# A Hedgehog attention mix on one core: raw K and Q weights by 128-partition transfers of one head per partition block, x0's low parts on VectorE, another order of V and the folds

## The chip, the core and the metric

The kernel runs on one core of a Trainium2 chip. Its engines have their own instruction queues and wait for each other by semaphores: PE (TensorE, matmuls; PEld is its weight load), DVE (VectorE), ACT (ScalarE), POOL (GpSimd), and SP (SyncE), which here only issues DMA transfers. The metric is device time in microseconds (us) of the launch, the median of several runs. The profile shows one further execution.

## The reference

Two attention branches, A and B, get the same `x` (2048 tokens of 448) and are mixed by a gate. All is float32.

```python
qkv = (x @ wqkv) -> q, k, v            # 16 heads of 28
pq, pk = q @ w_phi, k @ w_phi          # per head, 28 x 28
phi(p) = concat([softmax(p), softmax(-p)])
kv = einsum("bhsf,bhsd->bhfd", phi(pk), v);  z = sum over s of phi(pk)
o  = (phi(pq) @ kv) / (phi(pq) @ z + 1e-6)
out_branch = o.reshape(B, S, D) @ wo
g = sigmoid((x * gate_w).sum(-1));  result = g * out_A + (1 - g) * out_B
```

## The kernel before

**Precision.** A product of float32 matrices is made of three faster ones: each operand is split into a rounded high part (fp32r) and a low part, what is left (`low_part`, a subtraction of two SBUF tiles), and high*high, high*low and low*high are summed in PSUM. So each 448-row contraction is 11 matmuls (`mms`), and each projection of one tile of 128 tokens for one branch is a group of 11: VA and VB (V of branch A and B), K and Q.

**Folding.** K and Q are never computed raw. `fold` multiplies the raw weights (transposed, rows = head dimension) with `w_phi` once, so that the projections give the features directly. The raw weights lie in `wts[:, k, b, g]` (k: K or Q; b: branch; g: head within a block), a view of the tile `ret`: block q of four heads lies on the partitions 32q to 32q+27, and each of its four heads g is a row piece of 512 floats. One fold covers two of the four g (gh and gh+2) of one branch, for K and Q: 32 small matmuls of 28 rows into the PSUM tile `F` (the profile has two PE records for each), a 32x32 block transpose of F by DVE (`STREAM_TRANSPOSE`) into `ft` (two buffers, `ret` and `ru` in turn), then the high parts by ACT (rk for K, rq for Q) and the low parts by DVE or POOL. There are four folds, in program order F0 and F1 (branch A), F2 and F3 (branch B); F has one buffer. `wpd`, the other operand of the folds, comes from eight small transfers that POOL issues (`load_wp`).

**Loads.** `load_x0`, `load_wv`, `load_x` and half of `load_wt` are issued by SP in a single queue. The raw V weights are `wvr` (eight transfers, chunk c and branch b). The raw K and Q weights come as 16 transfers, one for each (k, b, q): 28 partitions, on each four pieces of 2 KB. For q = 0, 1 SP issues them, for q = 2, 3 POOL. A transfer waits on SP until the one issued eight before it has landed. The second branch's raw weights share memory with `wvr` and wait until that is read; the third pair of x tiles (`load_x(2)`, called x2 below, tokens 512 to 767) shares `xraw` with x0.

**Order.** `steps()` lists the work in the order that PE has to do it. `Plan.order` takes the cost, the latency and the dependences of each step, works out a due time for each (its lead `ahead` moves it earlier), and lists the instructions of the other engines accordingly; no run-time scheduler is behind it. `two` marks steps of DVE and POOL that the planner doesn't put beside each other.

**The start** is: `v_first` (V of the tiles 0 and 1 from x0, as the chunks of x0 and of the V weights land; V of tile 1 is put into the PSUM tile `K`), then VA and VB of the tiles 2, 3 and 4 with the folds among them, then K and Q of tile 0, K of tile 1, and from there a steady stream of K, Q, V and the accumulation of kv over the 16 tiles. The exponentials and normalisations of K are made by ACT, POOL and DVE (`k_soft`), those of Q after a turn through DRAM (`q_front`, `q_soft`). The last stage computes the numerators (`num`), mixes them and multiplies with `wo`.

**x0.** Chunk 0's low part and the mixed chunk's are made by DVE, those of the chunks 1 and 2 (128x512) by POOL.

Of the kernel before, what the change touches and what calls it, by code (L numbers as in the profile page):

```python
# [7 lines left out]
F32 = mybir.dt.float32  # L8
# [19 lines left out]
class Plan:  # L28
# [5 lines left out]
    def __init__(self):  # L34
        self.steps, self.writer, self.readers = [], {}, {}

    def add(self, eng, cost, fn, r=(), w=(), lat=0.1, kb=0, two=False, ahead=0.0):
# [10 lines left out]
        self.steps.append((eng, cost, lat, fn, deps, kb, two or eng == "POOL", ahead))  # L48

    def hand_over(self, old, new, fn=None):  # L50
        self.add("NONE", 0.0, fn, (), (*old, *new), lat=0.0)
# [56 lines left out]

def steps():

    yield from (("V01", 0, 0, 1), ("x1",), ("V01", 1, 0), ("V01", 1, 1), ("wq", 0), ("x", 2), ("wq", 1), ("V", 2), ("F", 0, 0, "DP"), ("V", 3, 0), ("F", 0, 1, "DP"))
    yield from (("V", 3, 1), ("V", 4, 0), ("F", 1, 0, "DD"), ("V", 4, 1), ("F", 1, 1, "DD"), ("later",), ("k", 0, 0), ("q", 0, 0), ("k", 0, 1), ("ks", 0), ("K", 1), ("wo_rows",))
    yield from (("q", 0, 1), ("qf", 0))
    yield from (("S", 0, JIT % 3 - 1), ("K", 2), ("Q", 1), ("S", 1, (JIT - 1) % 3 - 1), ("k", 3, 0), ("k", 3, 1), ("kv", 0, 1), ("ks", 3), ("V", 5))
    for p in range(2, 8):
        if p < 7:
            yield "x", p + 1
        yield "K", 2 * p
        yield "Q", 2 * p - 2
        if 2 * p - 2 < JIT:  # L120
            yield "S", 2 * p - 2, (JIT - 2 * p + 2) % 3 - 1
        if p == 7:
            yield "V", 14, 0
        yield "kv", 2 * p - 2, 2 * p - 1
        yield "wo", p - 2
        if p in (3,):
            yield "wo", 6
        if p < 6:
            yield "V", 2 * p + 2
        yield "K", 2 * p + 1  # L130
        if p < 7:
            yield "Q", 2 * p - 1
            if 2 * p - 1 < JIT:
                yield "S", 2 * p - 1, (JIT - 2 * p + 1) % 3 - 1
        if p < 6:
            yield "V", 2 * p + 3
        if p == 6:
            yield "gates", 0, 12
            yield "gates_b", 0, 12
    yield from (("load_wo",), ("V", 14, 1), ("Q", 13), ("V", 15), ("free_v",), ("free_k",), ("kv", 14, 15), ("free_e",), ("kv_turn",), ("gates", 12, NT))  # L140
    yield from (("fetch", 0, 2), ("fetch", 1, 3), ("Q", 14))
    kept, late = list(range(2, JIT - 2)), list(range(JIT, NT))
    rest = []
    while kept or late:
        rest.append((kept.pop(0) if kept else late.pop(0), late.pop(0) if late else kept.pop(0)))
    pairs = [((JIT - 1, JIT - 2), (0, 1)), ((0, 1), (2, 3))] + [(t, (2 * (i % 2), 2 * (i % 2) + 1)) for i, t in enumerate(rest)]
    for p, (tiles, slots) in enumerate(pairs):
        yield "num", tiles, slots
        if p == 0:
            yield from (("Q", 15), ("free_x",), ("free_q",))  # L150
        if p:
            for i, t in enumerate(pairs[p - 1][0]):
                yield "out", 2 * p - 2 + i, t, ("O0", "O1")[i]
        end = p == len(pairs) - 1
        yield "mix", p, ("DVE", "DVE") if end else ("POOL", "POOL"), ("T0", "T1"), ("DVE", "DVE") if end else ("POOL", "POOL")
        if p == 1:
            yield "gates_b", 12, NT, [("o", 2)]
        if p + 2 < len(pairs):
            for t, s in zip(*pairs[p + 2]):
                yield ("S" if t >= JIT else "fetch"), t, s  # L160
    for i, t in enumerate(pairs[-1][0]):
        yield "out", 2 * len(pairs) - 2 + i, t, ("O0", "O1")[i]
# [7 lines left out]
def hedgehog_mix(ctx: ExitStack, tc: tile.TileContext, xd, wv, wkt, wqt, wphi, wo, cmask, cpmask, out):  # L170
# [107 lines left out]
    def put(eng, n, fn, r, w, **k):  # L278
        add(eng, both(eng, n), fn, r, w, **k)

    def low_part(eng, n, o, a, h, r, w):
        put(eng, n, tt(eng, o, a, h, OP.subtract), r, w, two=eng == "DVE")

# [11 lines left out]
    def split_x0():  # L295
        n, t, f = 0, xs[0], xs[0].bitcast(F32)
        h, l = [[(k, n, i) for i in range(2)] for k in ("x", "xl")]
        put("ACT", 2 * P, act(t[:, 0], xraw[:, 0]), [("x0raw", 0)], [("x0h", 0)])
        low_part("DVE", 2 * P, t[:, 4], xraw[:, 0], f[:, 0], [("x0raw", 0), ("x0h", 0)], [("x0l", 0)])
        put("DVE", 6 * P, lambda: V.tensor_copy(t[:, 1:4], xraw[:, 1:]), [("x0raw", 1)], [("x0h", i) for i in (1, 2, 3)])  # L300
        low_part("DVE", 2 * P, t[64:P, 3], xraw[64:P, 3], f[64:P, 3], [("x0raw", 1)], [("x0h", 3)])
        low_part("POOL", 4 * P, t[:, 5:7], xraw[:, 1:3], f[:, 1:3], [("x0raw", 1), ("x0h", 1), ("x0h", 2)], [("x0l", i) for i in (1, 2)])

    def load_x(p):
        xraw, kr = raws[p]
        add("SP", 0.4, dma(xraw, xd[:, 2 * P * p:2 * P * p + 2 * P].rearrange("(c p) t -> p c t", p=P)), [], [(kr,)], lat=2, kb=512)

    def split_x(p, lo, hi, low, high="ACT", after=()):
        xraw, kr = raws[p]
# [9 lines left out]

    def load_wv(c, b):  # L320
        lo, hi = ((0, D + 2), (D + 2, 2 * D + 2))[b]
        add("SP", 0.4, dma(wvr[:, c, lo:hi], wv[c * P:(c + 1) * P, lo:hi]), [], [("wvr", c, b)], lat=2.5, kb=331, ahead=50.0 if c + b == 0 else 30.0 - 2 * (c + 4 * b))

    def split_wv(c, b, low):
        lo, hi = ((0, D + 2), (D + 2, 2 * D + 2))[b]
# [24 lines left out]
    def fold(b, gh, low):  # L350
        n = 2 * b + gh
        def mm():
            for l in range(2):
                g = 2 * l + gh
                for o in range(4):
                    for q in range(4):
                        nc.tensor.matmul(bank["F"][32 * o:32 * o + 32, q, 256 * l:256 * l + 256], wpd[32 * q:32 * q + DH, b, g],
                                         wts[32 * q:32 * q + DH, :, b, g].rearrange("p k (j o i) -> p o k j i", o=4, i=32)[:, o],
                                         start=True, stop=True)
        add("PE", 1.4, mm, [("wpd",), *[("wt", k, b, q) for k in range(2) for q in range(4)]], ["F"])  # L360
        f = ft[n % 2]
        add("DVE", 2.25, lambda: V.transpose(f.rearrange("p k j f u -> p (u k j f)"), bank["F"].rearrange("p k n -> p (k n)")),
            ["F"], [ftk[n % 2]], ahead=4.0 * (n == 3))
        for k, (wh, wl) in enumerate(((wkh, wkl), (wqh, wql))):
            for j in (0, 2):
                h, l = (x[:, j:j + 2, b, :, gh::2].rearrange("p j f u -> p j u f") for x in (wh, wl))
                s = f[:, k, j:j + 2, :FD].rearrange("p j f u -> p j u f")
                key = "kq"[k]
                add("ACT", 0.9, act(h, s), [ftk[n % 2]], [(key, "h", b, gh, j)], ahead=2.0 * (k == 0))
                e = "POOL" if low[k] == "P" or low[k] == "M" and j else "DVE"  # L370
                add(e, {"DVE": 0.88, "POOL": 1.4}[e], tt(e, l, s, h.bitcast(F32), OP.subtract), [ftk[n % 2], (key, "h", b, gh, j)], [(key, "l", b, gh, j)], two=e == "DVE")

    def wkeys(k, bs):
        return [(k, h, b, gh, j) for h in "hl" for b in bs for gh in range(2) for j in (0, 2)]
# [309 lines left out]
    def free_q():  # L684
        pools["q"].close()
        banks("three", "right", O1=1, T1=1)

    nums, outs, loaded = [0], [0], {}
    for what, *a in steps():
        if what == "V":  # L690
# [3 lines left out]
            v_first(a[0], a[1:])  # L694
        elif what in ("K", "k", "ks"):
            if what == "k" and a == [0, 0]:
                plan.hand_over([("x1raw",), *[("wt", k, 1, q) for k in range(2) for q in range(4)]], [("e", n, s) for n in range(NE) for s in range(2)])
            if what != "ks":
                for b in a[1:] or range(2):
                    k_proj(a[0], b)  # L700
# [21 lines left out]
        elif what == "x1":  # L722
# [4 lines left out]
        elif what == "wq":  # L727
            if a[0]:
                plan.hand_over([("wvr", c, b) for c in range(4) for b in range(2)], [("wt", k, 1, q) for k in range(2) for q in range(4)])
            for k in range(2):  # L730
                load_wt(k, a[0])
        elif what == "wo":
            split_wo(a[0])
        elif what == "num":
# [73 lines left out]
```

## Time and profile before

| | |
|---|---|
| median of 3 runs | 346.66 us (344.67 to 346.75) |
| the profiled execution | 345.97 us, span 344.2 us |
| busy share of the span | PE 97%, PEld 86%, DVE 83%, POOL 73%, ACT 42% |
| granted TensorE clock, mean | 0.995 |
| HBM read, written | 32.00 MB, 24.22 MB |
| first fold's matmuls, last fold's | 22.06 us, 39.88 us from the span's start |

A line of the timeline is: start in us, length in us, engine, line of the code, operation, out<-in, shapes, count; in brackets the idle time of the engine just before it, and what ended it. Neighbouring instructions of one kind are one row, so a group of 11 matmuls is one row with x11. PE's times are modelled at their ends: successive groups of 11 start 2.2 us apart where nothing holds them. A row of the stages is: from:to, length, then busy time (and count) of PE, PEld, DVE, ACT and POOL, the granted clock, the mean busy share of the 16 DMA engines, and GB/s. KB are of 1024 bytes.

### The profile page before, as it was taken

The numbers are of one execution on the slowest core, as the hardware profiler recorded it, in microseconds if no ns is written. First come the engines' busy times: TensorE is split into PE (matmuls) and PEld (weight loads), VectorE is DVE, ScalarE is ACT, GpSimd is POOL, SyncE is SP. The second block draws the span as 40 slices with busy tenths as digits, with TensorE's granted clock in tenths as the row PEclk, the third lists the DMA queues.
The fourth block names the chain that finished last, engine by engine and source line by source line (L and its number), as shares of the span: only waits on it lengthen the run. The fifth ranks groups of instructions, "written<-read, shape, count | busy, mean of one in ns | idle before, by whom it ended". The sixth has DMA issues, their size and how long they took to land.

```text
span 344.2 us, 8900 instructions
## 1 busy us (share of the span) xinstructions
PE 333.1 (97%) x3776; PEld 296.5 (86%) x3776; DVE 285.1 (83%) x338; ACT 143.7 (42%) x219; POOL 251.5 (73%) x211
## 2 busy tenths in 40 slices
PE   7889899999999999999999999999999999999995
PEld 6777587999999999999999999899878888788894
DVE  4608886997779769899998999997599999999960
ACT  4516743553444535364444452343043243433231
POOL 8426605899999799999996998697087778788500
PEclk9999989999999999999999999999999999999999
DMA  7995620550317756964735422376974545141011
GB/s 251 251 206 133 203 75 1 156 168 2 116 55 261 252 169 229 327 204 197 246 84 236 143 55 81 96 248 261 301 259 164 202 152 183 76 177 55 29 53 53
DMA packets 29262, 55.18 MB, mean 160 GB/s; under 512 B 4472, under 2 KB 23528, under 8 KB 26920
## 3 DMA queue, kind: packets, MB, share of 16 engines
q1 hardware_dynamic: 28328, 52.68, 47.6%
q0 software_dynamic: 896, 1.95, 2.6%
q8 instruction: 29, 0.48, 0.6%
q14 instruction: 9, 0.07, 0.1%
HBM read 32.00 MB, written 24.22 MB: 163 GB/s over the span
## 4 chain that ended last, share of the span: by engine, by line
POOL 30%; PE 24%; DVE 23%; DMA 10%; issue 8%; ACT 2%; SPq 1%; POOLq 0%; DVEq 0%; ACTq 0%
POOL ret L266 20%; PE O L630 10%; DVE ret L545 5%; DMA ret<-in_wqt 4%; PE K L409 3%; POOL rx L266 3%; PE Q L409 3%; DVE rv L593 3%; POOL rv L602 3%; PE N L582 2%; DVE sm L488 2%; DVE mx L481 2%; DVE qsm L540 2%; DMA wst<-wos 1%; DMA ret<-in_wv 1%
## 5 line engine op out<-in xcount | busy, mean ns | idle before, releaser
L409 PE MATMUL K<-rk,rx 128*128 128x432 f32 x352 | 74.0, 366 | 0.7 <-ACT pk L269 0.6
L409 PE MATMUL Q<-rq,rx 128*128 128x432 f32 x352 | 72.4, 360 | 0.2 <-DVE Q L672 0.2
L409 PEld LDWEIGHTS K<-rk,rx 128*128 128x128 f32 x352 | 67.1, 192 | 5.1 <-ACT pk L269 1.5
L630 PE MATMUL O<-rk,rx 128*128 128x448 f32 x336 | 70.6, 369 | 0.1
L630 PEld LDWEIGHTS O<-rk,rx 128*128 128x128 f32 x336 | 62.5, 188 | 8.5 <-ACT rx L621 1.2
L409 PEld LDWEIGHTS Q<-rq,rx 128*128 128x128 f32 x352 | 65.9, 188 | 4.4 <-PE K L409 0.7
L269 ACT ACTIVATE ret<-ret 128x896 f32<-128x896 f32 x48 | 45.7, 953 | 55.0 <-POOL ret L266 54.9
L266 POOL TENSOR_TENSOR ret<-ret,sm 128x896 f32<-128x896 f32 x32 | 53.9, 1707 | 8.1 <-DVE sm L489 8.1
L266 POOL TENSOR_TENSOR ret<-pk,mx 128x896 f32<-128x896 f32 x16 | 27.3, 1705 | 16.6 <-DVE mx L481 16.5
L488 DVE TENSOR_REDUCE sm<-ret 128x32 f32<-128x896 f32 x32 | 33.8, 1073 | 6.7 <-ACT ret L269 6.7
L545 DVE STREAM_TRANSPOSE ret<-ret 128x2048 f32<-128x2048 f32 x16 | 36.5, 2282 | 1.9 <-POOL ret L266 1.6
L540 DVE TENSOR_REDUCE qsm<-ret 128x32 f32<-128x896 f32 x32 | 33.4, 1055 | 3.0 <-ACT ret L269 2.7
L409 PE MATMUL VA<-rv,rx 128*128 128x450 f32 x154 | 34.7, 372 | 0.3 <-POOL rx L266 0.3
L409 PE MATMUL VB<-rv,rx 128*128 128x448 f32 x154 | 33.7, 366 | 0.0
L266 POOL TENSOR_TENSOR ret<-qmn,ru 128x896 f32<-128x896 f32 x16 | 28.2, 1765 | 5.3 <-DVE ret L545 4.2
L269 ACT ACTIVATE ret<-ru 128x896 f32<-128x896 f32 x16 | 15.2, 952 | 39.4 <-issue 17.3
L409 PEld LDWEIGHTS VA<-rv,rx 128*128 128x128 f32 x154 | 28.5, 189 | 3.6 <-POOL rx L266 0.7
L409 PEld LDWEIGHTS VB<-rv,rx 128*128 128x128 f32 x154 | 28.8, 188 | 3.0 <-issue 0.4
L266 POOL TENSOR_TENSOR ret<-mx,pk 128x896 f32<-128x896 f32 x16 | 27.3, 1706 | 1.5 <-DVE mx L482 1.5
L266 POOL TENSOR_TENSOR ret<-ret,qsm 128x896 f32<-128x896 f32 x16 | 27.3, 1705 | 0.9
L602 POOL TENSOR_TENSOR rv<-rv,rd 128x896 f32<-128x896 f32 x14 | 23.8, 1703 | 1.1
L534 DVE TENSOR_REDUCE qmn<-ru 128x32 f32<-128x896 f32 x16 | 16.9, 1058 | 6.7 <-DMA ru<-qd 6.6
(94 smaller groups left out, 445.1 us busy)
## 6 DMA issues: line engine op xcount, KB each, us to landing
ed<-ret SPq DMA_DIRECT2D x8, 1024.0 KB
ret<-ed SPq DMA_DIRECT2D x8, 1024.0 KB
qd<-ru SPq DMA_DIRECT2D x64, 112.0 KB
ru<-qd SPq DMA_DIRECT2D x16, 448.0 KB
out<-ret SPq DMA_DIRECT2D x16, 224.0 KB
wod<-wst SPq DMA_DIRECT2D x14, 224.0 KB
rk<-wod SPq DMA_DIRECT2D x2, 1568.0 KB
xraw<-in_xt SPq DMA_DIRECT2D x6, 512.0 KB
```

What stands on the lines that cost most here:

```text
L266: return lambda: ENG[eng].tensor_tensor(val(o), val(a), val(b), op)
L269: return lambda: A.activation(val(o), val(i), f, **k)
L409: nc.tensor.matmul(bank[name][:, k, lo:hi], x[:, xc, o:o + P], w[l][:, c], start=i == 0, stop=i == len(XT) - 1)
L481: put("DVE", 2 * D, lambda: V.tensor_reduce(mh[0], pkh, AX.X, OP.max), [kp], [km[0]])
L488: put("DVE", 2 * D, lambda s=s, e3=e3: V.tensor_reduce(sm[:, s], e3, AX.X, OP.add), [ke[s]], [("sm", t % 2, s)])
L534: put("DVE", 2 * D, lambda: V.tensor_reduce(qmn, tq.rearrange("p c b g f -> p c (b g) f"), AX.X, OP.min), [kt], [kn])
L540: put("DVE", 2 * D, lambda s=s, e3=e3: V.tensor_reduce(qsm[:, s], e3, AX.X, OP.add), [ke[s]], [("qsm", i, s)])
L545: add("DVE", 2.25, lambda: V.transpose(eTf[slot], eq.rearrange("p s a c f -> p (s a c f)")), ke, turned(slot))
L582: nc.tensor.matmul(bank["N"][32 * g:32 * g + 32, r, 2 * b * P:2 * b * P + 2 * P], kvt[32 * r:32 * r + 32, b, s, g], eTp[slots[0] // 2][32 ...
L593: add("DVE", 0.07 + 1.08 * nt, lambda: V.transpose(ctr().rearrange("p (r n) -> p r n", r=4), bank["N"][:, :, :2 * nt * P]), ["N"], [("ctr" ...
L602: put(eng, 2 * D, lambda: ENG[eng].tensor_tensor(mid["o", n % 3].rearrange("p (c a f) -> p a c f", c=4, a=8), ctv()[:, :, i, :, :DH], rd[: ...
L630: nc.tensor.matmul(bank[pb][:, 0, :D], a, w, start=i == 0, stop=i == len(terms) - 1)
```

## The change

- `load_wt(n)` now loads what fold n needs: for each of its two g and for K and Q one transfer, the piece of 512 floats of head g of all four blocks. The source pattern is four blocks (step 112 rows) of 32 rows of 512 floats, the destination all 128 partitions; the last four rows of each block belong to the next head and land on partitions that no matmul reads. For the very last head the fourth block would run past the tensor, so there it is split: three blocks of 32 rows, and 28 rows. That makes 18 transfers, all issued by SP; POOL issues none of them. Fold n waits for its own transfers alone.
- The low parts of x0's chunks 1 and 2 are made by DVE.
- `steps()`: F0 now stands right behind VA of tile 2, F1 behind VB of tile 2, F2 behind VB of tile 3, F3 behind VA of tile 4; VB of tile 4 comes after the first K group.
- Every fold's low parts of Q go to POOL, those of K to DVE (before, the second branch's all went to DVE).
- Planner numbers: the leads of x, the V weights, and the exponential of the gate's logit of the tiles 0 and 1; `two` is off for the folds' low parts.

```diff
-    yield from (("V01", 0, 0, 1), ("x1",), ("V01", 1, 0), ("V01", 1, 1), ("wq", 0), ("x", 2), ("wq", 1), ("V", 2), ("F", 0, 0, "DP"), ("V", 3, 0), ("F", 0, 1, "DP"))
...
+    yield from (("V01", 0, 0, 1), ("x1",), ("V01", 1, 0), ("V01", 1, 1), ("wt", 0), ("x", 2), ("wt", 1), ("wt", 2), ("wt", 3), ("V", 2, 0), ("F", 0, "DP"), ("V", 2, 1))
...
-        low_part("POOL", 4 * P, t[:, 5:7], xraw[:, 1:3], f[:, 1:3], [("x0raw", 1), ("x0h", 1), ("x0h", 2)], [("x0l", i) for i in (1, 2)])
+        low_part("DVE", 4 * P, t[:, 5:7], xraw[:, 1:3], f[:, 1:3], [("x0raw", 1), ("x0h", 1), ("x0h", 2)], [("x0l", i) for i in (1, 2)])
...
-    def load_wt(k, b):
-        rows = (wkt, wqt)[k][b].rearrange("(q g d) c -> q d g c", q=4, d=DH)
-        for q in range(4):
-            o, i, w = wts[32 * q:32 * q + DH, k, b], rows[q], [("wt", k, b, q)]
-            if q < 2:
-                add("SP", 0.2, dma(o, i), [], w, lat=2, kb=690)
-            else:
-                add("POOL", 0.6, lambda o=o, i=i: G.dma_start(o, i), [("vh", 2, 1)], w, lat=4 + 1.3 * (4 * b + 2 * k + q - 2), ahead=8.0 if b == 0 else 0.0)
+    def load_wt(n):
+        b, gh = divmod(n, 2)
+        for l in range(2):
+            for k in range(2):
+                g = 2 * l + gh
+                src, o = (wkt, wqt)[k], wts[:, k, b, g]
+                qs = ((0, 4),) if g < 3 or b == 0 else ((0, 3), (3, 4))
+                for lo, hi in qs:
+                    rows = HP if hi - lo > 1 else DH
+                    i = bass.AP(tensor=src.tensor, offset=src.offset + (D * b + 112 * lo + DH * g) * 512, ap=[[112 * 512, hi - lo], [512, rows], [1, 512]])
+                    add("SP", 0.4, dma(o[HP * lo:HP * lo + (hi - lo - 1) * HP + rows], i), [], [("wt", k, b, g if lo == 0 else 4)], lat=2, kb=229, ahead=20.0 - 4 * n)
...
-        add("PE", 1.4, mm, [("wpd",), *[("wt", k, b, q) for k in range(2) for q in range(4)]], ["F"])
+        add("PE", 1.4, mm, [("wpd",), *[("wt", k, b, g) for k in range(2) for g in ((0, 2), (1, 3), (0, 2), (1, 3, 4))[n]]], ["F"])
...
-            add("ACT", 0.2, act(glog[:, t:t + 1], lambda: bank[n_][:, k, D:D + 1], AF.Exp, scale=-1.0), [kb], [("gl", t)])
+            add("ACT", 0.2, act(glog[:, t:t + 1], lambda: bank[n_][:, k, D:D + 1], AF.Exp, scale=-1.0), [kb], [("gl", t)], ahead=9.0 * (t < 2))
```

On PE, from V of the tiles 1 (in the tile K) and 2 to the first groups of K and Q, the order before was as follows (F are the folds, 32x256 the shape of their outputs; VA, VB, K, Q groups of one projection):

```order
L441 MATMUL K<-rv,rx 128x448 x11
L409 MATMUL VA<-rv,rx 128x450 x11
L409 MATMUL VB<-rv,rx 128x448 x11
L357 MATMUL F<-ret,wpd 32x256 x32
L409 MATMUL VA<-rv,rx 128x450 x11
L357 MATMUL F<-ret,wpd 32x256 x32
L409 MATMUL VB<-rv,rx 128x448 x11
L409 MATMUL VA<-rv,rx 128x450 x11
L357 MATMUL F<-ret,wpd 32x256 x32
L409 MATMUL VB<-rv,rx 128x448 x11
L357 MATMUL F<-ret,wpd 32x256 x32
L409 MATMUL K<-rk,rx 128x432 x11
```

On PE, the same place in the changed kernel:

```order
L444 MATMUL K<-rv,rx 128x448 x11
L412 MATMUL VA<-rv,rx 128x450 x11
L360 MATMUL F<-ret,wpd 32x256 x32
L412 MATMUL VB<-rv,rx 128x448 x11
L360 MATMUL F<-ret,wpd 32x256 x32
L412 MATMUL VA<-rv,rx 128x450 x11
L412 MATMUL VB<-rv,rx 128x448 x11
L360 MATMUL F<-ret,wpd 32x256 x32
L412 MATMUL VA<-rv,rx 128x450 x11
L360 MATMUL F<-ret,wpd 32x256 x32
L412 MATMUL K<-rk,rx 128x432 x11
L412 MATMUL VB<-rv,rx 128x448 x11
```

F0 moved ahead of VB of tile 2, F3 directly behind VA of tile 4, and VB of tile 4 behind the first K group; the four folds keep their order.

On SP, before, from the load of x1 (into `ret`) to the load behind the weights (x3, the second one into `xraw`); wkt and wqt are the raw K and Q weights:

```order
L272 DMA ret<-in_xt 128x4x256
L272 DMA ret<-in_wkt 28x4x512 x2
L272 DMA ret<-in_wqt 28x4x512 x2
L272 DMA xraw<-in_xt 128x4x256
L272 DMA ret<-in_wkt 28x4x512 x2
L272 DMA ret<-in_wqt 28x4x512 x2
L272 DMA xraw<-in_xt 128x4x256
```

On SP, the changed kernel, the end of the same place: the last of the transfers for branch B, up to the load of x3 (into `xraw`). Ahead of these rows now stand x1, eight transfers of 128x1x512 (K and Q in turn), x2, and four more of 128x1x512:

```order
L272 DMA ret<-in_wkt 128x1x512
L272 DMA ret<-in_wqt 128x1x512
L272 DMA ret<-in_wkt 96x1x512
L272 DMA ret<-in_wkt 28x512
L272 DMA ret<-in_wqt 96x1x512
L272 DMA ret<-in_wqt 28x512
L272 DMA xraw<-in_xt 128x4x256
```

Eight transfers of 28 partitions on SP (and eight more on POOL) became 18 on SP, and x2 stands behind eight of them instead of behind four.

More of the change, by code (lines that the diff above doesn't have):

```diff
@@ L35, in __init__, with add @@
         self.steps, self.writer, self.readers = [], {}, {}
-    def add(self, eng, cost, fn, r=(), w=(), lat=0.1, kb=0, two=False, ahead=0.0):
+    def add(self, eng, cost, fn, r=(), w=(), lat=0.1, kb=0, two=None, ahead=0.0):
         i, deps = len(self.steps), set()
@@ L47, in add @@
             self.writer[k], self.readers[k] = i, set()
-        self.steps.append((eng, cost, lat, fn, deps, kb, two or eng == "POOL", ahead))
+        self.steps.append((eng, cost, lat, fn, deps, kb, eng == "POOL" if two is None else two, ahead))
     def hand_over(self, old, new, fn=None):
@@ L281, in low_part @@
     def low_part(eng, n, o, a, h, r, w):
-        put(eng, n, tt(eng, o, a, h, OP.subtract), r, w, two=eng == "DVE")
+        put(eng, n, tt(eng, o, a, h, OP.subtract), r, w, two=True)
     x1raw = re.rearrange("p e n -> p (e n)")[:, -8 * P:].rearrange("p (c t) -> p c t", c=4)
@@ L370, in fold @@
                 e = "POOL" if low[k] == "P" or low[k] == "M" and j else "DVE"
-                add(e, {"DVE": 0.88, "POOL": 1.4}[e], tt(e, l, s, h.bitcast(F32), OP.subtract), [ftk[n % 2], (key, "h", b, gh, j)], [(key, "l", b, gh, j)], two=e == "DVE")
+                add(e, {"DVE": 0.88, "POOL": 1.4}[e], tt(e, l, s, h.bitcast(F32), OP.subtract), [ftk[n % 2], (key, "h", b, gh, j)], [(key, "l", b, gh, j)], two=False)
     def wkeys(k, bs):
@@ L686, in free_q @@
         banks("three", "right", O1=1, T1=1)
+    wt1 = [("wt", k, 1, g) for k in range(2) for g in range(5)]
     nums, outs, loaded = [0], [0], {}
@@ L696, in hedgehog_mix @@
             if what == "k" and a == [0, 0]:
-                plan.hand_over([("x1raw",), *[("wt", k, 1, q) for k in range(2) for q in range(4)]], [("e", n, s) for n in range(NE) for s in range(2)])
+                plan.hand_over([("x1raw",), *wt1], [("e", n, s) for n in range(NE) for s in range(2)])
             if what != "ks":
@@ L726, in hedgehog_mix @@
             plan.hand_over([("x0" + k, i) for k in "hl" for i in range(4) if (k, i) != ("l", 3)], [(k, 0, i) for k in ("x", "xl") for i in range(2)])
[L727 to L731, printed above, removed]
+        elif what == "wt":
+            if a[0] == 2:
+                plan.hand_over([("wvr", c, b) for c in range(4) for b in range(2)], wt1)
+            load_wt(*a)
         elif what == "wo":
```

12 lines of the change are left out of this document (6 added, 6 removed).

## Prediction

> **What bounds the kernel now.** I read the stages first, then the chain that ended last, then PE's timeline. Columns of the stages: from:to, length, busy PE, PEld, DVE, ACT, POOL, granted clock, busy share of the 16 DMA engines, GB/s.
>
> ```profile
> 3.00:11.00 8.00, 6.71 (x91) 5.58 (x91) 5.63 (x8) 4.36 (x8) 7.72 (x15) 1.00 1.06 355
> 11.00:31.00 20.00, 18.39 (x199) 14.84 (x198) 7.50 (x10) 8.15 (x18) 5.75 (x8) 1.00 1.01 205
> 42.00:45.00 3.00, 3.00 (x10) 2.56 (x8) 2.68 (x2) 1.14 (x2) 0.00 (x0) 0.50 0.64 180
> 57.50:245.00 187.50, 187.26 (x1944) 174.71 (x1949) 165.26 (x201) 82.36 (x115) 164.50 (x113) 1.00 0.52 169
> ```
>
> From 57.5 to 245 us PE is busy 187.26 of 187.50 us: whatever moves the start of that stretch moves the end, as long as DVE and POOL (88% each there) shift with it; they take their input from PE's groups. So the change is priced by one number: when K of tile 2 begins, 57.56 us now. Ahead of it the DMA engines are full from 3 to 31 us, at 355 GB/s while 128-partition loads run and at 205 while the 28-partition K and Q weights run.
>
> The chain of waits (start, length, what) shows what PE waits for there:
>
> ```profile
> 8.70 14.70 DMA ret<-in_wqt
> 23.54 1.69 PE F L357 x58
> ```
>
> PE's timeline from V of tile 2 on:
>
> ```profile
> 17.51 2.40 PE L409 MATMUL VA<-rv,rx 128*128 128x450 f32 x11
> 19.74 2.38 PE L409 MATMUL VB<-rv,rx 128*128 128x448 f32 x11
> ...
> 23.54 1.69 PE L357 MATMUL F<-ret,wpd 28*32 28x256 f32 x62 [0.86 <-DMA ret<-in_wqt]
> ...
> 39.88 1.49 PE L357 MATMUL F<-ret,wpd 28*32 28x256 f32 x64 [1.66 <-DVE ret L362]
> ...
> 41.31 3.98 PE L409 MATMUL K<-rk,rx 128*128 128x432 f32 x11
> ...
> 45.51 2.40 PE L409 MATMUL Q<-rq,rx 128*128 128x432 f32 x11 [0.23 <-DVE Q L672]
> ...
> 57.56 4.59 PE L409 MATMUL K<-rk,rx 128*128 128x432 f32 x22
> ```
>
> A group of 11 costs 19.74 - 17.51 = 2.23 us. F0 waits for a raw Q weight until 23.5, F3 for a transpose until 39.88; then the first K group takes 3.98 us, since the clock stands at 0.50 there. F3 to K of tile 2 is 57.56 - 39.88 = 17.68 us.
>
> **The K and Q transfers, the term that decides.** The new ones carry 128 x 512 x 4 B = 262 KB each, 16 heads' worth (two of them in pieces). They would fill the memory like the loads that ran at 355 GB/s, if they use all DMA engines. Whether they do, a stretch behind the weights tells (packets, then issues: kind of transfer, count, KB each):
>
> ```profile
> DMA packets 1722, 2.39 MB, mean 154 GB/s; under 512 B 184, under 2 KB 1720, under 8 KB 1720
> ...
> xraw<-in_xt SPq DMA_DIRECT2D x1, 512.0 KB
> wos<-in_wo SPq DMA_DIRECT2D x2, 196.0 KB
> ...
> wst<-wos SPq DMA_DIRECT2D x1, 224.0 KB
> ...
> wos<-in_wo SPq DMA_DIRECT2D x2, 28.0 KB
> ```
>
> Between 33 and 48.5 us SP issued 16 transfers: one of x and one of wst with 128 rows outermost, and 14 of wos, two each of 28, 24, 20, 16, 12, 8 and 4 rows (7 KB a row, 196 down to 28 KB). Their rows are pieces of 1 KB (x) and 1.8 KB (the rest), so the 184 packets under 512 B are not data; I take them for what ends a transfer. With sixteen a transfer there would be 256. With the largest number up to 16 that divides the rows it is 2 x 16 + 2 x (14 + 12 + 10 + 16 + 12 + 8 + 4) = 184, exactly. So I read: a transfer is cut along its outermost dimension into equal shares, one a DMA engine, and 4 rows give 4 engines.
>
> The new source pattern is [4 blocks][32 rows][512], its destination [128 partitions][512]. A share must be cut on both sides, so I take 4 engines (3 for the two pieces of three blocks). Here both sides of each transfer had the same outermost number, so no row shows which side decides, nor that it is the same four engines every time; both are for the rivals.
>
> [...]
>
> What lies ahead of them in the queue (count, KB each):
>
> ```profile
> xraw<-in_xt SPq DMA_DIRECT2D x2, 512.0 KB
> ret<-in_wv SPq DMA_DIRECT2D x4, 225.0 KB
> ret<-in_wv SPq DMA_DIRECT2D x4, 224.0 KB
> ...
> ret<-in_wqt POOLq DMA_DIRECT2D x4, 224.0 KB, 9.6
> ...
> ret<-in_xt SPq DMA_DIRECT2D x1, 512.0 KB
> ...
> xraw<-in_xt SPq DMA_DIRECT2D x1, 384.0 KB
> ...
> xraw<-in_xt SPq DMA_DIRECT2D x1, 128.0 KB
> wp<-in_wphi POOLq DMA_DIRECT2D x8, 14.0 KB, 5.0
> ```
>
> x0 (512 KB), the V weights (1796), x1 (512) and wphi (112) are 2932 KB, 3.0 MB; 8 us at 355 GB/s move 2.84, and a little has moved before 3 us. So x1 is through at about 11 us. One engine does 355 / 16 = 22.2 GB/s; a quarter of 262 KB takes it 2.95 us. Four transfers a fold: F0's are in at 11 + 11.8 = 22.8, F1's at 34.6. Then x2, a sixteenth an engine, 32.8 KB, 1.5 us: 36.1. F2's at 47.9, F3's at 59.7. F3 begins at 59.8 instead of 39.88: **+19.9 us**.
>
> Bounds of the rate: above, the 355 of the 128-partition loads; below, the 205 of the 28-partition weights, 12.8 GB/s an engine and 5.1 us a transfer, which puts F3 at 11 + 16 x 5.1 + 2.6 = 95 us. I take the upper row, since here too every partition is written.
>
> **The order around the folds.** Behind F3 now stand the K group, VB of tile 4 and then Q: one group more than before, **+2.2**. VA and VB of the tiles 2 and 3 and VA of tile 4 (11 us) fill the waits between the folds, for nothing. The clock: before, it fell to 0.50 for the first K group (3.98 instead of 2.23, 1.75 us) after a wait of 1.66. In front of F3 PE would now be idle some 8 us (VA of tile 4 ends at 47.9 + 1.4 + 2.2 = 51.5). I keep the same 1.75; without a drop it is 1.75 less, with the fold (41.31 - 39.88 = 1.43) slowed too 1.4 more.
>
> **V's start, x0 on DVE, the gate's exponential.**
>
> ```profile
> 1.72 4.80 POOL L336 DMA_DIRECT2D wp<-in_wphi  x8 [0.71 <-DVE wpd L337]
> ...
> 6.82 2.17 DVE L266 TENSOR_TENSOR rv<-ret,rv 128x450 fp32r<-128x450 f32 x1 [0.49 <-ACT rv L269]
> 7.21 1.29 POOL L266 TENSOR_TENSOR rx<-xraw,rx 128x512 fp32r<-128x512 f32 x1
> 9.05 0.47 PE L441 MATMUL VA<-rv,rx 128*128 128x450 f32 x1 [1.13 <-DVE rv L266]
> 13.05 0.62 DVE L266 TENSOR_TENSOR rv<-ret,rv 128x448 fp32r<-128x448 f32 x1 [0.80 <-ACT rv L269]
> 15.14 2.53 PE L441 MATMUL K<-rv,rx 128*128 128x448 f32 x11 [0.74 <-ACT glog L269]
> ```
>
> DVE's subtraction took 2.17 us beside POOL's, 0.62 alone. On DVE the 128x512 part costs 0.62 x 512 / 448 = 0.71; PE's wait of 1.13 goes, and with the exponential ahead the 0.74 too. VA of tile 2 begins at about 15.4 instead of 17.51. On DVE wpd now stands ahead of the last three low parts of the V weights and waits for wphi, issued until 6.5 and 5.0 us on its way (its row above): until 11.5, about 1 us later than those parts could start, which VB of tile 0 would wait for. All this, 1 to 2 us, is worth nothing while F0 waits until 22.8: **0**.
>
> **POOL, DVE and SP.**
>
> ```profile
> 29.08 1.04 POOL L314 CAST rx<-xraw 128x1024 fp32r<-128x1024 f32 x1 [9.79 <-DMA xraw<-in_xt]
> 29.10 1.82 DVE L266 TENSOR_TENSOR rk<-ret,rk 128x432 fp32r<-128x432 f32 x1 [1.52 <-ACT rk L269]
> 30.20 3.24 POOL L266 TENSOR_TENSOR rx<-xraw,rx 64x256 fp32r<-64x256 f32 x2
> 33.90 3.58 POOL L266 TENSOR_TENSOR rq<-ret,rq 128x432 fp32r<-128x432 f32 x2
> 37.51 2.32 DVE L362 STREAM_TRANSPOSE ret<-F 128x2048 f32<-128x2048 f32 x1 [1.26 <-POOL rq L266]
> ...
> 44.35 0.92 DVE L266 TENSOR_TENSOR rk<-ret,rk 128x432 fp32r<-128x432 f32 x1 [0.32 <-PE K L409]
> 54.01 1.70 POOL L266 TENSOR_TENSOR ret<-pk,mx 128x896 f32<-128x896 f32 x1 [13.95 <-DVE mx L481]
> ```
>
> POOL gets four more low parts of Q, 7.2 us at 3.58 a pair; its idle 13.95 ahead of the first softmax covers them, and the Q group that needs F3's stands six groups (13 us) behind F3: 0. In the forecast x2 lands at 36, its split takes 1.04 + 3.24, the low parts of F0 and F1 7.2: done at 48, ahead of the transposes of F2 and F3: 0. On SP x3 and the wos loads queue behind the weights, on the same DMA engines, and shift with the rest; x3 is for the tiles 6 and 7, wos for a split that comes after the first softmax. If the weights come fast, this cover is gone, and DVE's low parts at 1.8 beside POOL push the transpose of F2 back (second paragraph of the rivals).
>
> Sum: 345.97 + 19.9 + 2.2 = **368 us**, for the profiled execution, 0.7 below the median of the runs, which changes nothing here.
>
> **The rivals.** *All sixteen engines* (the destination's 128 decides, or the four change from transfer to transfer, eight being in flight). Then at 355 GB/s F0's weights are in at 14, F1's at 17, x2 at 18.4, F2's 21.4, F3's 24.3; no fold waits for data, and V's start counts. PE: VA of tile 2 at 15.4 to 16.4, F0 at 17.6 to 18.6; I take the earlier. DVE: transpose to 21.3; the low part that POOL's split of x2 stretches, and F1's transpose, until 26.3; three low parts at 1.2 to 2.1, until 31.5; F2's transpose until 33.8, which F3 waits for. F3 at 33.8 is 6.1 earlier, VB costs 2.2, the slow clock's 1.75 may go: 345.97 - 5.6 = 340 us, 337 without DVE's delay (F3 at 31), 342 with the slow clock. It speaks for it that all loads with 128 partitions ran at 355; against it that 184 packets follow the outermost number, and the source's is 4. It decides from the point where F3's weights land by 37.5: 4.7 MB in 26.5 us, 178 GB/s, eight engines.
>
> *Four engines at the lower rate*: they collide on their way into the partitions, as the 28-partition weights seem to (205 GB/s at a share of 1.01). F3 at 95: 345.97 + 55 + 2 = 403 us.
>
> *About eight engines*: F3 near 37.7, no change, 346 us.
>
> **How the numbers follow.** Forecast 0.60 (361 without the clock's drop and with engines a tenth faster than 22.2 GB/s, 379 with the fold slowed and engines a fifth slower), all sixteen 0.28, lower rate 0.07, eight 0.05. The forecast's own range is 361 to 379. For 8 in 10 the range has to reach into the case of the other sign: 338 to 377. Faster by over 1% (what a measurement here tells from no change) 0.28, same 0.05, slower 0.67.
>
> **What would show it.** Right: F0 near 23, F1 near 35, F2 near 48 and F3 near 60 us, each waiting for a transfer of wkt or wqt; about 90 GB/s at a quarter of the DMA share between 11 and 59; K of tile 2 near 79. Wrong: 300 GB/s or more there, and F3 waiting for DVE before 35. The DVE subtraction at 0.62 and no wait for the exponential show the small terms in either case.

## The result, and the profile after

The changed kernel takes 364.22 us (median of 4 runs, 363.03 to 366.44); the kernel before, beside it, 345.67 us (342.83 to 346.75). The ratio is 1.056, 95% interval 1.047 to 1.065: slower. The profiled execution took 363.03 us (before 345.97), its span is 361.2 us (before 344.2), its mean granted clock 0.965 (before 0.995).

The stages of the changed kernel, columns as before (from:to, length, busy PE, PEld, DVE, ACT, POOL, granted clock, DMA share, GB/s):

```profile
3.00:11.00 8.00, 7.60 (x94) 6.53 (x94) 4.96 (x9) 3.79 (x7) 4.28 (x10) 1.00 1.02 342
14.00:22.00 8.00, 5.12 (x55) 4.04 (x53) 0.62 (x2) 2.22 (x5) 1.47 (x2) 0.98 0.26 102
33.00:58.00 25.00, 15.92 (x195) 11.26 (x196) 10.52 (x7) 7.82 (x12) 13.56 (x11) 0.70 0.38 129
74.50:262.00 187.50, 187.25 (x1937) 174.49 (x1948) 165.14 (x201) 82.15 (x114) 164.50 (x113) 1.00 0.52 169
```

Up to 11 us the loads run much as before (342 GB/s, before 355). Then the K and Q weights come, at 102 GB/s and a DMA share of 0.26. PE is busy 15.92 of the 25 us from 33 to 58 us. The last row is the twin of 57.5 to 245 us before: 187.5 us long, 187.25 of them busy, only 17 us later.

PE's timeline of the changed kernel, the folds and what follows (a fold is two rows of 32 where it is broken by a wait):

```profile
16.09 2.39 PE L412 MATMUL VA<-rv,rx 128*128 128x450 f32 x11
18.41 0.71 PE L360 MATMUL F<-ret,wpd 28*32 28x256 f32 x32
22.78 1.17 PE L360 MATMUL F<-ret,wpd 28*32 28x256 f32 x32 [3.65 <-DMA ret<-in_wqt]
23.88 4.47 PE L412 MATMUL VB<-rv,rx 128*128 128x448 f32 x11
...
33.53 1.17 PE L360 MATMUL F<-ret,wpd 28*32 28x256 f32 x32 [4.26 <-DMA ret<-in_wqt]
...
45.15 0.88 PE L360 MATMUL F<-ret,wpd 28*32 28x256 f32 x32 [3.26 <-DMA ret<-in_wqt]
...
55.88 1.34 PE L360 MATMUL F<-ret,wpd 28*32 28x256 f32 x32 [4.45 <-DMA ret<-in_wqt]
57.14 3.38 PE L412 MATMUL K<-rk,rx 128*128 128x432 f32 x11
60.36 2.38 PE L412 MATMUL VB<-rv,rx 128*128 128x448 f32 x11
...
74.55 4.59 PE L412 MATMUL K<-rk,rx 128*128 128x432 f32 x22
```

The waits of PE in the changed kernel, summed (what waited, for what: us in total, times, longest):

```profile
PE F L360 <- DMA ret<-in_wqt: 16.5, 5, 4.5
```

So all four folds wait for a raw Q weight, 16.5 us together, and K of tile 2 begins at 74.55 us instead of 57.56: 17.0 us later. The span is 17.0 us longer too (361.2 - 344.2). A time of F "at 55.88" below means its second half, which is the one that needs the last weights.

DVE's timeline of the changed kernel at V's start:

```profile
6.78 0.63 DVE L266 TENSOR_TENSOR rv<-ret,rv 128x450 fp32r<-128x450 f32 x1 [0.27 <-ACT rv L269]
7.32 1.14 DVE L266 TENSOR_TENSOR rx<-xraw,rx 128x512 fp32r<-128x512 f32 x2
...
11.35 0.38 DVE L266 TENSOR_TENSOR wpd<-wp 128x216 f32<-128x216 f32 x1 [0.71 <-DMA wp<-in_wphi]
```

The subtraction that took 2.17 us beside POOL's now takes 0.63, VA of tile 2 begins at 16.09 instead of 17.51, and none of it reaches the end, since F0 waits until 22.78.

### The profile page after: what moved, and what is told of

Read it like the earlier page. It is cut to its first block, busy times and chain, and to the rows that moved or that the text cites. A ratio compares the mean times of both kernels' runs of the same rounds, so it can differ in the third digit from the quotient of the medians.

```text
span 361.2 us, 8892 instructions
## 1 busy us (share of the span) xinstructions
PE 338.2 (94%) x3776; PEld 299.3 (83%) x3776; DVE 280.1 (78%) x335; ACT 142.9 (40%) x219; POOL 251.1 (69%) x206
## 4 chain that ended last, share of the span: by engine, by line
PE 60%; DVE 12%; DMA 8%; POOL 7%; SPq 6%; issue 5%; ACT 1%; POOLq 0%; DVEq 0%; ACTq 0%
PE Q L412 16%; PE K L412 14%; PE O L633 10%; PE VA L412 7%; PE VB L412 7%; DMA ret<-in_wqt 7%; SPq L272 6%; PE T L503 4%; POOL ret L266 3%; DVE rv L596 3%; POOL rv L605 3%; DVE ret L548 3%; PE N L585 2%; DMA ret<-in_wv 2%; DVE sm L491 1%
## 5 line engine op out<-in xcount | busy, mean ns | idle before, releaser
L491 DVE TENSOR_REDUCE sm<-ret 128x32 f32<-128x896 f32 x32 | 33.8, 1075 | 6.2 <-ACT ret L269 6.1
L412 PE MATMUL VA<-rv,rx 128*128 128x450 f32 x154 | 37.7, 397 | 0.0
L412 PE MATMUL VB<-rv,rx 128*128 128x448 f32 x154 | 35.5, 381 | 0.0
L412 PEld LDWEIGHTS VA<-rv,rx 128*128 128x128 f32 x154 | 31.2, 207 | 4.3 <-issue 1.4
L412 PEld LDWEIGHTS VB<-rv,rx 128*128 128x128 f32 x154 | 30.5, 199 | 3.3 <-issue 0.8
L360 PE MATMUL F<-ret,wpd 28*32 28x256 f32 x256 | 7.4, 482 | 16.7 <-DMA ret<-in_wqt 16.5
```

The costliest lines, as they stand in the source:

```text
L412: nc.tensor.matmul(bank[name][:, k, lo:hi], x[:, xc, o:o + P], w[l][:, c], start=i == 0, stop=i == len(XT) - 1)
L491: put("DVE", 2 * D, lambda s=s, e3=e3: V.tensor_reduce(sm[:, s], e3, AX.X, OP.add), [ke[s]], [("sm", t % 2, s)])
```

## Experiments

The first question was whether the number of blocks in the source pattern makes the transfers slow (theory), or something else that came with them: all transfers on SP's one queue, the layout of the weights in DRAM, 128 partitions written at once (rivals).

**128 rows outermost.** The weights already come to the kernel transposed and cut; here the same host code also lays the 128 rows that one transfer needs one behind the other (the four rows of the next head included). PE's order, the SP queue and everything else are those of the changed kernel, but for the split of the last head: 16 transfers instead of 18. No work is left out.

```diff
-                    i = bass.AP(tensor=src.tensor, offset=..., ap=[[112 * 512, hi - lo], [512, rows], [1, 512]])
-                    add("SP", 0.4, dma(o[...], i), [], [("wt", k, b, g if lo == 0 else 4)], ...)
+                add("SP", 0.4, dma(o, src[b, g, 0]), [], [("wt", k, b, g)], lat=2, kb=229, ahead=20.0 - 4 * n)
...
+    def gaps(w, blocks, pad):
+        a = rows(w).T.reshape(4, 112, 512)
+        a = _np.concatenate([a, a[:, :4]], axis=1)
+        a = _np.stack([a[:, 28 * g:28 * g + 32] for g in range(4)]).reshape(4, blocks, 128 // blocks, 512)
+        return _np.concatenate([a, a[:, :, :pad]], axis=2) if pad else a
...
-    wkt = _np.stack([rows(w[:, 448:896]).T for w in (wa, wb)])
+    wkt = _np.stack([gaps(w[:, 448:896], 1, 0) for w in (wa, wb)])
```

> The changed kernel with one difference: the raw K and Q weights lie in DRAM in the order in which they are to land, so the source pattern of each of the 16 transfers has 128 rows outermost instead of 4 blocks of 32 (the destination, the queue, the count up to the one split, PE's order are the same). If the source's outermost number of 4 held the transfers to 4 engines: some 340 GB/s or more between 13 and 25 us, no fold waits for a transfer, the last fold begins at 31 to 34 us, and the time is 337 to 342 us. If the layout of one head per block, SP as the only queue or the order of the folds is what costs: about 364 us, the folds waiting as before.

**Eight blocks, four blocks.** The same layout, but with a row left free behind every 16 or every 32 rows, so that the source pattern keeps 8 or 4 blocks outermost. The edit is shown for 8, against the kernel with 128 rows. The one with 4 is the control: if the layout were what helped, it would be fast.

```diff
-                add("SP", 0.4, dma(o, src[b, g, 0]), ...)
+                add("SP", 0.4, dma(o, src[b, g, :, :16]), ...)
...
-    wkt = _np.stack([gaps(w[:, 448:896], 1, 0) for w in (wa, wb)])
+    wkt = _np.stack([gaps(w[:, 448:896], 8, 1) for w in (wa, wb)])
```

> As the run with 128 rows, but the rows lie in DRAM in 8 blocks of 16 with a gap of one row behind each, so that the source pattern has 8 outermost. If the outermost number sets the engines: 8 times 25.5 GB/s, 204 GB/s, between 13 and 30 us, the last fold's weights in at about 34 us, and a time within 1% of the 128 rows' or up to 2 us above it. If a DMA queue, not the engines, is what limits: 102 GB/s or 350, not between.

> The control for both: the same DRAM layout with a gap, but 4 blocks of 32 rows. If the outermost number decides: 102 GB/s, the last fold's second half at 55.9 us, 364 us. If the reordered rows in DRAM are what makes the loads fast: the time of the 128 rows' run.

| kernel | us, median (runs) | ratio to before, 95% interval | F3 | K of tile 2 |
|---|---|---|---|---|
| changed kernel | 364.22 (4) | 1.056 [1.047, 1.065] | 55.88 | 74.55 |
| 128 rows | 342.61 (10) | 0.991 [0.988, 0.994] | 32.69 | 51.04 |
| 8 blocks | 346.43 (8) | 1.002 [0.998, 1.006] | 36.99 | 56.51 |
| 4 blocks | 365.95 (2) | 1.058 [1.048, 1.067] | 55.45 | 74.86 |

The times of F3 and of K of tile 2 come from one traced execution each; with 8 blocks it was the slowest of the eight, 350.38 us.

The stage from 14 to 22 us (the last two columns are DMA share and GB/s), with 4 blocks:

```profile
14.00:22.00 8.00, 4.81 (x53) 3.79 (x52) 0.31 (x1) 1.97 (x5) 1.47 (x2) 1.00 0.26 102
```

with 8 blocks, in which x2 (128 rows outermost) falls into this stage, and below it the stage from 27 to 31 us, in which the weights run alone:

```profile
14.00:22.00 8.00, 7.38 (x95) 5.83 (x94) 1.98 (x2) 1.93 (x5) 1.48 (x2) 1.00 0.68 217
27.00:31.00 4.00, 3.40 (x46) 2.45 (x44) 3.87 (x3) 3.43 (x6) 3.84 (x5) 1.00 0.53 204
```

and with 128 rows, x2 among them:

```profile
14.00:22.00 8.00, 8.00 (x97) 6.55 (x95) 2.69 (x2) 2.21 (x5) 3.92 (x5) 1.00 1.06 401
```

102, 204 and 401 GB/s are 25.5, 25.5 and 25 GB/s an engine with 4, 8 and 16 engines, and the shares of 0.26 and 0.53 are about 4 and 8 of 16. The destination had 128 partitions each time, the queue and the bytes were the same, and with 4 blocks the new layout is as slow as the old one. So here it is the outermost number of the source that decides, and the same few engines serve all transfers in flight: in the changed kernel SP had issued seven of them by 19.6 us, before F0's four had landed, and four engines that changed from one transfer to the next would have added up to more than 102. The small packets say the same. The changed kernel from 13 to 23 us (packets, MB, rate; then how many are small), 3.9 transfers of 262 KB with 4 small packets each:

```profile
DMA packets 516, 1.02 MB, mean 102 GB/s; under 512 B 16, under 2 KB 16, under 8 KB 516
```

The destination's number was never varied, so these runs don't show what it does by itself; nor does any trace here show which of the 16 engines serve, only that they stay the same.

With 128 rows no fold waits for data any more; F3 waits 0.42 us for a transpose on DVE. PE's timeline of that kernel:

```profile
28.33 1.49 PE L356 MATMUL F<-ret,wpd 28*32 28x256 f32 x64
29.75 2.52 PE L408 MATMUL VA<-rv,rx 128*128 128x450 f32 x11
32.69 1.49 PE L356 MATMUL F<-ret,wpd 28*32 28x256 f32 x64 [0.42 <-DVE ret L361]
34.12 2.43 PE L408 MATMUL K<-rk,rx 128*128 128x432 f32 x11
36.39 2.38 PE L408 MATMUL VB<-rv,rx 128*128 128x448 f32 x11
...
51.04 4.59 PE L408 MATMUL K<-rk,rx 128*128 128x432 f32 x22
```

It is faster than both kernels (by 0.9% against the kernel before). With 8 blocks the time was 3.8 us above it, more than I had expected. There the first three folds wait 0.6 to 1.0 us for their last weight, and F3 then 2.67 for DVE's transpose, which had itself waited 1.25 us for a low part on POOL; behind that wait the first K group takes 3.98 us, as in the kernel before, and the granted clock between 33 and 58 us is 0.93 in both, against 1.00 with 128 rows. PE's timeline with 8 blocks:

```profile
36.99 1.56 PE L356 MATMUL F<-ret,wpd 28*32 28x256 f32 x64 [2.67 <-DVE ret L361]
38.48 3.98 PE L408 MATMUL K<-rk,rx 128*128 128x432 f32 x11
```

**V's start alone**, put into the kernel before, whose transfers and order stay. The second line of the edit in words: the exponential of the gate's logit of the tiles 0 and 1 gets its lead.

```diff
-        low_part("POOL", 4 * P, t[:, 5:7], xraw[:, 1:3], f[:, 1:3], ...)
+        low_part("DVE", 4 * P, t[:, 5:7], xraw[:, 1:3], f[:, 1:3], ...)
```

> The kernel before with the small parts of the change alone: x0's low parts on DVE and the lead of the gate's exponential for the tiles 0 and 1; the loads, the folds and their order stay. My sum has it at nothing, since the first fold waits for its weights until 23.5 us: VA of tile 2 begins 1 to 2 us earlier than 17.5, the first fold at 23.5 as before, 345 to 347 us. If the start of V counts, the time falls by those 1 to 2 us.

345.87 us (10 runs), ratio 0.998 [0.995, 1.002]. K of tile 2 began at 56.11, 1.45 us earlier, but the time doesn't show it. Conversely, x0's low parts back on POOL in the kernel with 128 rows:

> The kernel with 128-row transfers, x0's low parts of chunks 1 and 2 back on POOL. Theory: here no fold waits for data, so V's start counts: POOL holds DVE's first subtraction up again (2.17 instead of 0.63 us), VA of tile 2 begins 1.3 us later, K of tile 2 at about 52.3 instead of 51.04, and the time is 1.3 us longer, 343.9. Rival: the delay is taken up by waits for DVE further on (F3 waits 0.4 us for a transpose) or by the numerators: the same 342.6.

342.53 us (12 runs), ratio 0.992 [0.988, 0.995], against 0.991 with them on DVE: no difference that can be measured, where I had expected 1.3 us. K of tile 2 began at 51.50 instead of 51.04, one trace each. So where nothing waits for weights the move shows 0.5 us in the traces and nothing in the times.

**The order of VB of tile 4.** First in the changed kernel:

```diff
-    yield from (..., ("V", 4, 0), ("F", 3, "DP"), ("later",), ("k", 0, 0), ("V", 4, 1), ("q", 0, 0), ...)
+    yield from (..., ("V", 4, 0), ("V", 4, 1), ("F", 3, "DP"), ("later",), ("k", 0, 0), ("q", 0, 0), ...)
```

> The kernel after, with the whole V of tile 4 ahead of F3 again (VB of tile 4 no longer between the K and the Q group behind it). Theory of the forecast: F3 waits for its weights until 55.9 us in any order, so VB of tile 4 (2.2 us) fits in that wait: K of tile 2 moves from 74.55 to about 72.3 and the time from 364.2 to 362. Rival: the group only moves; F3 is late by as much because PE gets to it later, or the clock's slow piece moves behind F3: 364, K of tile 2 within 0.5 of 74.5.

363.06 us (4 runs), ratio 1.051 [1.045, 1.056]; K of tile 2 at 73.05 instead of 74.55. So VB of tile 4 fits in the wait for F3's weights, as the theory says, but it brings 1.5 us in the trace rather than 2.2, and 1.2 in the medians, whose intervals overlap. Some of the difference stands at the K group behind F3: 3.38 us in the changed kernel, it takes 4.33 here. PE's timeline:

```profile
55.39 1.34 PE L360 MATMUL F<-ret,wpd 28*32 28x256 f32 x32 [3.43 <-DMA ret<-in_wqt]
56.66 4.33 PE L412 MATMUL K<-rk,rx 128*128 128x432 f32 x11
60.78 2.62 PE L412 MATMUL Q<-rq,rx 128*128 128x432 f32 x11
```

Then the whole order of PE put back to that of the kernel before, where the weights are fast (128 rows, and 10 small matmuls instead of 30, which the next part explains):

```diff
-    ... ("V", 2, 0), ("F", 0, "DP"), ("V", 2, 1), ("F", 1, "DP"), ("V", 3, 0), ("V", 3, 1), ("F", 2, "DP"), ("V", 4, 0), ("F", 3, "DP"), ("later",), ("k", 0, 0), ("V", 4, 1), ("q", 0, 0), ...
+    ... ("V", 2, 0), ("V", 2, 1), ("F", 0, "DP"), ("V", 3, 0), ("F", 1, "DP"), ("V", 3, 1), ("V", 4, 0), ("F", 2, "DP"), ("V", 4, 1), ("F", 3, "DP"), ("later",), ("k", 0, 0), ("q", 0, 0), ...
```

> The kernel with 128-row transfers and 10 small matmuls, with PE's order of V and the folds put back to that of the kernel before (VA and VB of tile 2 ahead of F0, VA of tile 3 ahead of F1, VB of tile 3 and VA of tile 4 ahead of F2, VB of tile 4 ahead of F3). Theory: F3 comes when DVE and PE have done the same work in either order, so F0 is 2.2 us later, F3 up to 2.2 us later and K of tile 2 the same, 50.9 plus or minus 0.5; time 340.3. Rival: the earlier folds of the new order are what gains: DVE gets F0 2.2 us later and stays behind, K of tile 2 at 53, time 342.5.

343.69 us (12 runs), ratio 0.997 [0.994, 0.999], against 340.32 us and 0.984 [0.980, 0.989] for the same kernel with the new order: my theory was wrong, the order is worth about 3 us here. K of tile 2 began at 52.87 instead of 50.92. PE's timeline with the old order:

```profile
34.64 1.49 PE L356 MATMUL F<-ret,wpd 28*32 28x256 f32 x64 [0.51 <-DVE ret L361]
36.06 2.44 PE L408 MATMUL K<-rk,rx 128*128 128x432 f32 x11
40.83 2.40 PE L408 MATMUL Q<-rq,rx 128*128 128x432 f32 x11 [2.33 <-DVE Q L671]
```

F3 was 2 us later than with the new order (32.69 with 128 rows), and VB no longer behind it should have made up for that. But then Q's first group waits 2.33 us for a memset of its PSUM tile, which stands on DVE behind F3's transpose. With VB between K and Q that wait is nearly covered (0.22 us). In the kernel before it was 0.23 us because the K group ahead of it took 3.98 us, at a granted clock of 0.57; with V's start alone K took 2.43 us, and Q waited 1.34. The time differs by some more than the 1.95 us of K of tile 2; 1.2 us of the rest is a longer wait of a later Q group for `ru` (1.67 against 0.43 us, near 210 us), whose cause stays open.

**Where 3 us of the gain with 128 rows went.** By the forecast's rule an earlier K of tile 2 is carried to the end. With 128 rows it was 6.5 us earlier, the profiled time only 3.3 (342.70 against 345.97). PE's timeline of that kernel, at the first numerators (N, 128 matmuls; "issue" is a wait for nothing that the profile shows):

```profile
237.93 2.74 PE L581 MATMUL N<-ret,kvt 32*32 32x256 f32 x127
242.90 0.40 PE L581 MATMUL N<-ret,kvt 32*32 32x256 f32 x1 [2.23 <-issue]
```

In the kernel before, the 128 matmuls run through:

```profile
243.91 2.75 PE L582 MATMUL N<-ret,kvt 32*32 32x256 f32 x128
```

The gap stands in the kernels with 8 and 4 blocks too, also behind the 127th, at 247.5 and 264.2 us (and at 242.6 in the one with x0's low parts on POOL). What they have in common is not the time but the count of what PE had done, here from the start to a point in the gap (PE and PEld busy, with counts). With 128 rows:

```profile
0.00:240.80 240.80, 237.82 (x2521) 216.28 (x2521) 196.67 (x238) 110.41 (x161) 190.96 (x148) 1.00 0.54 178
```

with 8 blocks:

```profile
0.00:247.60 247.60, 238.52 (x2521) 216.40 (x2521) 198.25 (x238) 109.44 (x161) 191.24 (x148) 0.99 0.52 172
```

with 4 blocks:

```profile
0.00:264.40 264.40, 244.87 (x2521) 220.81 (x2521) 197.11 (x238) 110.36 (x161) 191.55 (x148) 0.95 0.49 161
```

A queue of its own moves packets of 16 KB, in the page of the changed kernel (packets, MB):

```profile
q8 instruction: 29, 0.48, 0.6%
```

PE executes 7552 matmuls and weight loads, 260 for each of the 29 packets, and from the end of the first packet to the end of the last 7186, 257 for each of 28: I take these for PE's instructions, in blocks. A group of N uses up 256 of them in 2.7 us. So the theory: PE has run out of instructions, and the next block is late. A packet of this queue stands in the gap: with 128 rows it runs from 240.59 to 241.51 us. The rival: the last matmul of N waits for data. At the very start the kernel runs 30 small matmuls of zeros, which no output needs; by the theory, leaving some out moves every later instruction within its block.

```diff
-WARM, SMALL = 10, 30
+WARM, SMALL = 10, 10
```

> The kernel with 128-row transfers, 20 of the 30 small matmuls of zeros that stand ahead of V's first group left out (0.3 us of work that no output needs, 80 instructions of PE's stream in the trace's count). The 2.2 us in which the last matmul of the first N group waits for nothing the trace shows: if PE has then run out of instructions (a block of 256 of them comes as a packet of 16 KB during that gap), the end of what it holds moves 80 instructions later, past the Q group behind it, and the packet has 4.6 us more: the gap goes, K of tile 2 stays at 51, and the offset of -6.0 us against the kernel before is carried through the N groups: about 340.3, 2 us less than with 30. Rival: the gap belongs to the data that N reads: it stays where it is, at the end of the group, time 342.6.

> The same kernel with 20 more small matmuls instead (50). If PE runs out of instructions, the gap moves 80 instructions, that is 40 matmuls, forward: it falls in the middle of the first N group, behind about 86 of its 128 matmuls, and lasts longer, since the packet comes at the same time: 3 us instead of 2.2. Rival (data): the gap stays in front of the last matmul, 2.2 us.

> The kernel with 128-row transfers and 28 of the small matmuls of zeros instead of 30 (4 matmul records and 4 weight loads fewer). With 30 PE stood still after 2521 matmuls and 2521 weight loads, behind 127 of the 128 matmuls of the first N group, and so it did in the kernels with 8 and with 4 blocks, 7 and 24 us later in time. If it runs out of instructions there, the count decides: it stops after 2521 again, which is now 3 matmuls into the Q group behind N, for about 2 us. Rival (the last matmul of N waits for data): the stop stays in front of N's 128th matmul, after 2517.

> The same with 32 (4 matmul records more). If PE runs out of instructions: a stop after 2521 matmuls again, which is now behind 123 of the 128 of the first N group, for about 2 us. Rival (data): in front of the 128th, after 2525.

With 10 the gap is gone, and the time is 340.32 us (340.13 to 340.94, 4 runs), ratio 0.984 [0.980, 0.989]: the fastest kernel of this study. PE's timeline with 10:

```profile
238.40 2.76 PE L581 MATMUL N<-ret,kvt 32*32 32x256 f32 x128
```

With 50 it is gone too (341.83 us, 2 runs), where I expected it in the middle of N: the block came sooner there than I had assumed. The small steps decide it. With 28, PE's timeline, a stop 3 matmuls into the Q group:

```profile
237.76 2.76 PE L581 MATMUL N<-ret,kvt 32*32 32x256 f32 x128
240.45 0.86 PE L408 MATMUL Q<-rq,rx 128*128 128x432 f32 x3
242.35 4.00 PE L408 MATMUL Q<-rq,rx 128*128 128x432 f32 x19 [1.04 <-issue]
```

and with 32, behind 123 matmuls of N:

```profile
239.62 2.71 PE L581 MATMUL N<-ret,kvt 32*32 32x256 f32 x123
243.31 0.62 PE L581 MATMUL N<-ret,kvt 32*32 32x256 f32 x5 [0.99 <-issue]
```

Both stop after 2521 matmuls again, at the places expected to the matmul, for 1.0 us instead of 2 (one run each, 340.58 and 343.44 us). A wait for data would have stayed at its matmul. In all six kernels that stop there PE goes on 1.3 to 1.5 us after such a packet has ended (with 128 rows at 242.90, after 241.51; with 28 at 242.35, after 240.96; with 32 at 243.31, after 241.96). In the other traces the packet had ended earlier, 1.7 us or more before PE got to that count (2.0 with 10, 3.2 in the kernel before). That fits a block that is late. What sets when its packet is sent stays open.

Last, the kernel before with V's start alone, now with 10 small matmuls, since a gap of 1.74 us in its second N group might have hidden the gain:

> The kernel before with V's start alone changed (the run v_start), with 10 small matmuls instead of 30. Theory: its K of tile 2 came 1.45 us earlier than before, and 1.7 us of that was lost in a gap of the N stage in which PE had run out of instructions; 80 instructions fewer move the end of what PE holds behind the next Q group, the gap goes and the time is 343.8 to 344.2, against 345.9 with 30. Rival: the gap stays or comes back at another N group: 345.9.

The gap went, but the median is 345.77 (12 runs), ratio 1.001 [0.996, 1.005]; 344 had been expected. So V's start alone gains nothing that can be measured in the kernel before. In the traced execution (344.30 us) K of tile 2 even began at 53.87, 3.7 us earlier than before, and the time was only 1.7 us shorter; 1.5 us of that went to a Q group that waits for `ru` near 211 us, where the kernel before has no wait. Between the two traces with V's start alone, which differ in the small matmuls only, K of tile 2 differs by 2.2 us, so a single trace says little about a shift of that size.

## Why the prediction was right

The direction and the time were right: 368 us forecast, range 338 to 377, 364.22 measured. The deciding step, four engines for a source of four blocks, was argued from 184 small packets of transfers with equal sides; the runs with 4 blocks, 8 blocks and 128 rows showed it. By the steps:

- **The rate of an engine was the mis-sized term.** The forecast took 22.2 GB/s, a sixteenth of the 355 of the loads ahead; measured were 25.5. The folds' weights were due at 22.8, 34.6, 47.9 and 59.8 us and came at 22.78, 33.53, 45.15 and 55.88. The first agrees by luck, since two errors cancel: four quarters of 262 KB at 25.5 GB/s take 10.3 us (from F0 to F1 it is 10.75), so by that they began near 12 to 12.5 us, not 11. The term is +16.0 us (55.88 - 39.88) instead of +19.9. The 355 was read off loads in rows of 1 and 1.8 KB; the new rows are 2 KB, and with 128 of them 16 engines did 401; that the length of the rows is the reason was not tested.
- **VB of tile 4 behind F3 and the clock.** F3 to K of tile 2 was to take 17.68 + 2.2 = 19.9 us; it took 74.55 - 55.88 = 18.67. Of the 1.2 us, 1.0 stands at the first K group: to the next group it is 60.36 - 57.14 = 3.22 us, instead of 45.51 - 41.31 = 4.20 before, in which Q's wait of 0.23 is contained. The fold gave 0.2 (57.14 - 55.88 = 1.26 instead of 1.43): half of it had been done before the wait, but the other half ran at a granted clock of 0.50. The clock was low behind the other three waits as well (0.50 in VB of tile 2, which took 4.47 us, 0.51 and 0.60 in the groups behind F1 and F2), which cost nothing, since the next fold waited anyway.
- **Carried to the end.** K of tile 2 came 17.0 us later, and 345.97 + 17.0 = 363.0 is the measured profile. That every shift there reaches the end was too strong a rule, though: it held in this kernel, while in the traces with 128 rows and 8 blocks the N stage took back 3 to 4 us.
- **Worth nothing: V's start, POOL, DVE and SP.** Right. `wpd` began at 11.35 us (11.5 forecast), VA of tile 2 at 16.09 (15.4 to 16.4). From F0 to K of tile 2 PE waits for the weights and, behind them, for ACT (0.63 us, as before), for nothing else over 0.2 us. V's start alone moved no measurable time in the kernel before, nor did its x0 part in the kernel with 128 rows.
- **The rivals.** All sixteen engines: F3 at 33.8 with a wait for DVE, 340 us; the kernel with 128 rows had F3 at 32.69, waiting for DVE, and 342.6, or 340.3 without the stop in N. Eight engines: F3 at 37.7, 346 us; measured 36.99 and 346.4, in part by luck, since F3 waited there for DVE's transpose and not for its weights. So the wrong sign would have come with a layout of 128 rows, by the mechanism that the rival described.

## What to carry to other kernels

Before you merge small transfers into large ones, look at the outermost dimension of the transfer's source pattern: here 128 partitions from a source of 4 blocks ran at 102 GB/s, and the same bytes from 128 equally spaced rows at 401. Where one engine has no gap for most of the kernel, price a change in the start by the first group of that stretch, and then look for stretches with many short instructions, where part of the gain can go. A group moved behind a wait costs up to its length (1.5 of 2.2 us here, in the trace), but one that covers the next wait (VB between K and Q) can earn it back, so what an order is worth depends on where the waits are.

## What the runs showed of the hardware that I had not expected

- PE can run out of instructions, by all that these runs show: in a group of 128 short matmuls (21 ns each), or 3 matmuls behind it, it stopped for 1.0 to 2.3 us, after 2521 matmuls and 2521 weight loads in six kernels, whether that was at 240.7, 247.5 or 264.2 us, and went on 1.3 to 1.5 us after a packet of 16 KB had ended. Four matmul records more or fewer at the start moved the place by exactly four matmuls; 40 fewer or more took the stop away.
- An engine's rate hardly depended on how many of them worked: 25.5 GB/s with 4 and with 8, 25 with 16 (401 GB/s in all).
- After waits of 3 to 4.5 us the granted clock of PE fell again and again in the changed kernel, to a mean of 0.70 between 33 and 58 us, and groups of 11 that take 2.2 us took 3.2 to 4.5. The length of the wait alone doesn't decide: behind 1.66 us in the kernel before the clock fell to 0.50, behind 2.33 us in the one with the old order and fast weights Q took 2.40 us, and the clock was 1.00 in the mean of the whole execution.
